# A long-convolution and MLP kernel: second transform stages in 64-row tiles, in-place products, 32x32 turns on VectorE, a 128-row last stage and a token-major gate

## The chip, the cores and the metric

The kernel runs on one core of a Trainium2 chip. The metric is device microseconds of one execution; of several executions the median is given. The engines are named as the profile names them: PE (TensorE matmul) with PEld (its weight loads), DVE (VectorE), ACT (ScalarE), POOL (GpSimd) and SP (SyncE, which issues DMAs).

## The reference

All tensors are bf16, S = 2048 tokens, D = 512 channels, a hidden width of 1376. Cut to what matters:

```
h  = x + LN(x) * y            # x = A_q, LN without scale and shift
kv = shift_conv(k, 4 taps) * v
y  = causal_conv(kv, ssm_k) + kv * ssm_D     # per channel, length 2048, by FFT in fp32
h2 = h + relu(LN(h) @ w1) @ w2
```

The reference pads the convolution to 4096 points, takes real FFTs of kv and ssm_k along the tokens, multiplies them and transforms back; the first 2048 results are y.

## The kernel before

Everything is on chip; the work is a chain of stages, and the program order of each engine is written out by hand (`manual_schedule`), so an instruction waits for everything in front of it on its own engine. PSUM and SBUF tiles come from pools with a fixed number of buffers; a tile's next use waits for the last reader of the old one.

The transform of a channel's 2048 tokens, t = 64 a + b, is done in two matmul stages at odd frequencies. `to_rows` (L220) turns the channel-major input so that the 32 values of a lie on partitions: 64 transposes of 128x128 on PE, evacuated by DVE and ACT in turns. `stage1` (L226) contracts over a in four 32-row tiles that run side by side (tile_position 32 rg), with a bf16 high and a bf16 low part of the sine table, and writes 64 columns: 32 frequencies k1, real and imaginary. For x (not for k) it streams 128 columns, of which the upper 64 are zeros (`wide`). Its results go to `a1k` and `a1x`, with partitions (d, b): d is a half of a 128-channel group. Between the stage-1 groups of k, `taps` (L272) makes the four-tap shift convolution as matmuls with diagonal matrices `wdiag` and DVE multiplies with v.

`stage2` (L243) contracts over b with 128x128 tables `cc`, `cs`, `cn` (cosine, sine, minus sine) that are block diagonal in d: half of each table is zeros. For k it gives the real part and the imaginary part separately into `kf`; the real part gets ssm_D added (L306). For x the `product` (L328) multiplies both parts with both parts of kf, split 176 to 80 channels between DVE (from PSUM) and POOL (from a copy that ACT makes), and `finish` (L346), two steps behind, sums the four products on PE with plus and minus identity matrices into `psy`, which ACT copies back into kf. A step handles two k1; there are 16.

`inv1` (L474) contracts over the second frequency with `dre` and `dim`, 16 blocks of eight N=256 matmuls, evacuated by ACT and DVE into `ax`. Beside it lie the tables of the last stage (`ec_turns`, `ec_wrap`, `ec_sins`), the first LayerNorm (`ln1_stats`, `ln1_norm`), DMA transposes of x and of LN(x) into channel-major `xT` and `qT` (`lift`, `rows_T`), and the subtraction of the mean over D from w1 (`column_means`, `center`), which stands in for the mean of the second LayerNorm. `inv2` (L531) is the last stage: 512-column groups of channel-major results from 32-row tiles, four side by side, 128 matmuls for each quarter q. `gate` (L522) multiplies with qT and adds xT, all channel-major, so `mlp1` takes its result straight from SBUF; a DMA transpose brings the sum back to token-major `xh` for the residual. `mlp1` and `mlp2` follow for each quarter, with inv2 of a later quarter between them.

Of the kernel before, what the change touches and what calls it, by code (L numbers as in the profile page):

```python
# [20 lines left out]
class _Pools:  # L21
# [13 lines left out]
    def pop(self, name):  # L35
        self.open.pop(name).__exit__(None, None, None)
# [5 lines left out]
def _turns(nc, out, r, col, M, quarter):  # L42

    nc.vector.tensor_scalar(out=out, in0=r, scalar1=col, scalar2=float(M // 2 + (M // 4 if quarter else 0)),
                            op0=ALU.mult, op1=ALU.add)
    nc.vector.tensor_single_scalar(out=out, in_=out, scalar=M - 1, op=ALU.bitwise_and)


def _tokens(src2d, t0, nt):

    D = src2d.shape[1]
    return [bass.AP(tensor=src2d.tensor, offset=src2d.offset + (16 * a + t0) * D, ap=[[64 * D, 32], [1, nt * D]])
            for a in range(4)]
# [3 lines left out]
def kernel(  # L57
# [22 lines left out]
    lo, hi = slice(0, 64), slice(64, 128)  # L80
    halves = (lo, hi)
# [4 lines left out]
    slotA = pl.push("slotA")  # L86
    vp = pl.push("vp")
    early = pl.push("early")
    wp = pl.push("wp", side="right")
    kvp = pl.push("kvp", side="right")  # L90
# [3 lines left out]
    sk = early.tile([P, DC, S], BF16, name="sk")  # L94
# [3 lines left out]
    dtab = consts.tile([P, 64, DC], BF16, name="dtab")  # L98
    draw = consts.tile([P, DC, 64], BF16, name="draw")
    for dp in range(2):  # L100
        src = bass.AP(tensor=A_ssm_D.tensor, offset=A_ssm_D.offset + 64 * dp, ap=[[0, 64], [P, DC], [1, 64]])
        nc.scalar.dma_start(out=draw[64 * dp:64 * dp + 64, :, :], in_=src)
    vT = vp.tile([P, DC, S], BF16, name="vT")
    CH = 512
    kT = [(kvp if c < 2 else early).tile([P, DC, CH + 16], BF16, name=f"kT{c}") for c in range(4)]
    wdiag = kvp.tile([P, DC, KS, P], BF16, name="wdiag")

# [10 lines left out]
    nbias = consts.tile([P, 1], F32, name="nbias")  # L118
    pbias = consts.tile([P, 1], F32, name="pbias")
    nc.vector.memset(nbias[:], -0.5 * TURN)  # L120
    nc.vector.memset(pbias[:], 0.5 * TURN)
    eps_t = consts.tile([P, 1], F32, name="eps_t")
    nc.vector.memset(eps_t[:], EPS)

    hsc = consts.tile([P, 2], F32, name="hsc")
    hbi = consts.tile([P, 2], F32, name="hbi")
    for t_, v_ in ((hsc, TURN / 8192), (hbi, -0.5 * TURN)):
        nc.vector.memset(t_[:], 0.0)
        for dp in range(2):
            nc.vector.memset(t_[halves[dp], dp:dp + 1], v_)  # L130
# [6 lines left out]
    n1i = early.tile([P, 1], I32, name="n1i")  # L137
    for s in range(0, P, 32):
        nc.gpsimd.iota(n1i[s:s + 32, :], pattern=[[0, 1]], base=0, channel_multiplier=1)
    r1 = early.tile([P, 32], I32, name="f1_r")  # L140
# [4 lines left out]
    r2 = early.tile([P, 32, 64], I32, name="w_r")  # L145
    nc.gpsimd.iota(r2[:], pattern=[[2, 32], [128, 64]], base=1, channel_multiplier=0)
    r3 = early.tile([P, 64], I32, name="dm_r")
    nc.gpsimd.iota(r3[:], pattern=[[1, 64]], base=0, channel_multiplier=0)
# [5 lines left out]
    n1c = early.tile([P, 1], F32, name="n1c")  # L154
    n2c = early.tile([P, 1], F32, name="n2c")
    nc.vector.tensor_copy(out=n1c[:], in_=n1i[:])
    nc.vector.tensor_copy(out=n2c[:], in_=n2i[:])

    t1 = early.tile([P, 64], I32, name="f1_t")
    _turns(nc, t1[:, 0:32], r1[:], n1c[:], 128, True)  # L160
    _turns(nc, t1[:, 32:64], r1[:], n1c[:], 128, False)
    f1f = early.tile([P, 64], F32, name="f1_f")
    _sin(f1f[:, 0:32], t1[:, 0:32], 128)
    _sin(f1f[:, 32:64], t1[:, 32:64], 128, neg=True)


    def pieces(name, *sizes):
        got, at = [], 0
        for i, n in enumerate(sizes):
            got.append((at, wp.tile([P, n, P], F32R, tag=f"{name}{i}", name=f"{name}{i}")))  # L170
            at += n
        return got

    cc, cs, cn = pieces("c2c", 16, 16), pieces("c2s", 22, 10), pieces("c2n", 8, 8, 8, 8)

    def at_k1(tab, k1):
        a, t = [p for p in tab if p[0] <= k1][-1]
        return t[:, k1 - a, :]

    tsn = early.tile([P, 32, 64], I32, name="w_ts")  # L180
    _turns(nc, tsn[:], r2[:], n2c[:], 8192, False)

    def table(dst, turns):
        for a, t in dst:
            for dp in range(2):
                nc.scalar.activation(out=t[:, :, 64 * dp:64 * dp + 64], in_=turns[:, a:a + t.shape[1], :], func=ACT.Sin,  # L186
                                     scale=hsc[:, dp:dp + 1], bias=hbi[:, dp:dp + 1])

    table(cs, tsn)
    f1hi = consts.tile([P, P], BF16, name="f1_hi")  # L190
    f1lo = consts.tile([P, P], BF16, name="f1_lo")
    for f in (f1hi, f1lo):
        nc.gpsimd.memset(f[:, 64:128], 0.0)
    nc.vector.tensor_copy(out=f1hi[:, 0:64], in_=f1f[:])
    f1d = early.tile([P, 64], F32, name="f1_d")
    nc.vector.tensor_tensor(out=f1d[:], in0=f1f[:], in1=f1hi[:, 0:64], op=ALU.subtract)
    nc.vector.tensor_copy(out=f1lo[:, 0:64], in_=f1d[:])
    _turns(nc, r2[:], r2[:], n2c[:], 8192, True)
# [3 lines left out]
    for a, b in ((0, 8), (8, 16), (16, 22), (22, 24), (24, 32)):  # L202
        (ao, to), (ai, ti) = [[p for p in tab if p[0] <= a][-1] for tab in (cn, cs)]
        nc.gpsimd.tensor_single_scalar(out=to[:, a - ao:b - ao, :], in_=ti[:, a - ai:b - ai, :].bitcast(F32), scalar=-1.0,  # L204
                                       op=ALU.mult)


    nc.gpsimd.tensor_copy(out=dtab[:], in_=draw[:].rearrange("p r g -> p g r"))

# [16 lines left out]
    def stage1(fl, a_out, gb, engs, wide=False):  # L226

        pss = [bank2("ps1") for _ in range(2)]
        outs = [pss[rg // 2][:, rg % 2, :] for rg in range(4)]
        for gi in range(8):  # L230
            for f, first in ((f1hi, True), (f1lo, False)):
                for rg in range(4):
                    rows = slice(32 * rg, 32 * rg + 32)
                    w = 128 if wide and gi < 7 else 64
                    nc.tensor.matmul(out=outs[rg][:, 64 * gi:64 * gi + w],  # L235
                                     lhsT=fl[rows, 8 * gb + gi, :, :].rearrange("p d n -> p (d n)"),
                                     rhs=f[rows, 0:w], start=first, stop=not first,
                                     tile_position=(32 * rg, 0), skip_group_check=True)
        for h in range(2):
            copy(engs[h], a_out[:, :, 32 * gb:32 * gb + 32].rearrange("p c (g r) -> p c g r", r=DC)[:, :, :, 2 * h:2 * h + 2],  # L240
                 pss[h][:].rearrange("p r (g c) -> p c g r", c=64))

    def stage2(ps, a_in, kp, s):  # L243

        for kk in range(2):
            k1 = 2 * kp + kk
            w_re, w_im = ((cc, cs), (cn, cc))[s]
            nc.tensor.matmul(out=ps[:, kk, :], lhsT=at_k1(w_re, k1), rhs=a_in[:, k1, :], start=True, stop=False,  # L248
                             skip_group_check=True)
            nc.tensor.matmul(out=ps[:, kk, :], lhsT=at_k1(w_im, k1), rhs=a_in[:, 32 + k1, :], start=False, stop=True,  # L250
                             skip_group_check=True)


    kfl = early.tile([P, 64, 2, 64], BF16, name="kfl")
    skv = sk[:].rearrange("p c (a b) -> p c a b", b=64)
    for q in range(8):
        to_rows(skv, q, kfl, "DADADADA"[q])
    table(cc, r2)

    t3 = early.tile([P, 2, 64], I32, name="dm_t")  # L260
    _turns(nc, t3[:, 0, :], r3[:], n2c[:], 64, True)
    _turns(nc, t3[:, 1, :], r3[:], n2c[:], 64, False)
    dsc = early.tile([P, 2, 64], F32, name="dm_f")
    _sin(dsc[:], t3[:], 64)
    dre = consts.tile([P, 2, 2, 64], F32R, name="dre")
    dim = consts.tile([P, 2, 2, 64], F32R, name="dim")
    nc.gpsimd.memset(dre[:].bitcast(F32), 0.0)
    nc.gpsimd.memset(dim[:].bitcast(F32), 0.0)
    a1k = slotA.tile([P, 64, 256], F32R, tag="A", name="a1k")

# [9 lines left out]

    for gb in range(8):
# [82 lines left out]
    for kp in range(16):  # L364
        product(kp)
        if kp >= LAG:
            finish(kp)
# [277 lines left out]
```

## Time and profile before

| what | value |
|---|---|
| median of 3 runs | 232.25 us (232.03 to 232.39) |
| span of the profiled execution | 230.8 us; the median of the runs lies 1.45 us above it |
| mean granted TensorE clock | 0.974 of full speed |
| busy: PE, PEld, DVE, ACT, POOL | 201.4, 142.4, 142.9, 118.1, 78.3 us |
| matmuls | 2544, each with a weight load |
| DMA | 20.10 MB, 49194 packets |

The span runs from the first to the last instruction of one execution. Busy time is the time in which an engine has at least one instruction under way; matmuls are pipelined, so their mean duration (N=512: 0.38 us) is longer than the distance from one to the next (0.23 us). A line of the groups gives line number, engine, operation, out<-in, shapes, count, then busy us and mean ns of one, then the idle time of the engine just before them with what ended most of it.

### The profile page before, as it was taken

How to read it: one execution, taken by the hardware profiler on the slowest of the kernel's cores; microseconds unless marked ns; L12 is line 12 of the kernel's file. 1: busy time of each engine (PE TensorE's matmuls, PEld its weight loads, DVE VectorE, ACT ScalarE, POOL GpSimd, SP SyncE). 2: the span in 40 equal slices, each digit the busy share in tenths (PEclk: the TensorE clock that was granted, in tenths of full speed). 3: DMA queues.
4: the chain of work that ended last, by engine and by line, in shares of the span. 5: the costliest groups of instructions: out<-in, count | busy, mean ns of one | idle time of the engine just before them, and what ended most of it. 6: DMA issues, size and time to landing. Idle time of an engine off the chain costs nothing.

```text
span 230.8 us, 5978 instructions
## 1 busy us (share of the span) xinstructions
PE 201.4 (87%) x2544; PEld 142.4 (62%) x2544; DVE 142.9 (62%) x214; ACT 118.1 (51%) x177; POOL 78.3 (34%) x108
## 2 busy tenths in 40 slices
PE   0485999899966699999898889999999999999991
PEld 0473454899955699998787775444744474444440
DVE  7974667676664589998685869583971346134031
ACT  3789766555585478888486501750162026206400
POOL 6399910000000599998860770400220002002000
PEclk9999999999999589999999997999999999999998
DMA  6999920000000000772962168977244214021011
GB/s 197 306 230 161 169 60 3 0 4 0 0 7 6 3 1 0 182 244 77 211 119 53 33 214 127 213 140 114 54 91 96 55 37 91 6 59 27 3 46 46
DMA packets 49194, 20.10 MB, mean 87 GB/s; under 512 B 44208, under 2 KB 47632, under 8 KB 49168
## 3 DMA queue, kind: packets, MB, share of 16 engines
q1 hardware_dynamic: 46688, 18.24, 37.7%
q10 hardware_dynamic: 2480, 1.48, 2.4%
q8 instruction: 20, 0.33, 0.6%
q14 instruction: 6, 0.05, 0.1%
HBM read 7.08 MB, written 2.10 MB: 40 GB/s over the span
## 4 chain that ended last, share of the span: by engine, by line
PE 78%; ACT 8%; DMA 4%; DVE 4%; POOL 3%; issue 2%; POOLq 0%
PE ps1m L552 17%; PE ps2m L565 16%; PE pz L540 7%; PE psy L351 6%; PE pst L223 5%; PE pkv L276 5%; PE u L248 4%; PE u L250 4%; DMA sk<-in_A_ssm_k_dram 4%; PE ps2k L248 3%; PE ps2k L250 3%; PE ps L235 3%; ACT a1x L213 3%; PE psi L479 2%; ACT c2c L186 2%
## 5 line engine op out<-in xcount | busy, mean ns | idle before, releaser
L554 ACT ACTIVATE h1T<-ps1m 128x512 bf16<-128x512 f32 (+1 forms) x44 | 26.0, 596 | 57.6 <-PE ps1m L552 57.6
L552 PE MATMUL ps1m<-xT,w 128*128 128x512 bf16 (+1 forms) x176 | 40.3, 390 | 0.0
L565 PE MATMUL ps2m<-w,h1T 128*128 128x512 bf16 (+1 forms) x176 | 38.7, 379 | 0.0
L568 DVE SCALAR_TENSOR_TENSOR o<-ps2m,rstd,xh 128x512 bf16<-128x512 f32 x16 | 12.0, 750 | 38.8 <-PE ps2m L565 38.7
L552 PEld LDWEIGHTS <-w 128*128 128x128 bf16 (+1 forms) x176 | 17.8, 102 | 21.1 <-issue 2.2
L341 DVE TENSOR_TENSOR t<-u,kf 128x704 fp32r<-128x704 f32 x32 | 27.1, 888 | 5.3 <-ACT usb L337 5.3
L341 POOL TENSOR_TENSOR t<-usb,kf 128x320 fp32r<-128x320 f32 x32 | 28.6, 923 | 4.2 <-ACT usb L337 3.2
L565 PEld LDWEIGHTS <-h1T 128*128 128x128 bf16 (+1 forms) x176 | 17.2, 98 | 20.7
L429 POOL TENSOR_SCALAR rstd<-mv 128x4 f32<-128x4 f32 x8 | 1.9, 241 | 66.4 <-DVE mv L427 66.3
L425 DVE BATCH_NORM_STATS2 st<-xh 128x6 f32<-128x512 bf16 x32 | 19.7, 676 | 0.0
L213 ACT CAST kf<-psy 128x512 fp32r<-128x512 f32 x30 | 17.5, 643 | 1.8 <-PE psy L351 0.2
L540 PE MATMUL pz<-ecore,ax 32*128 32x256 f32 (+7 forms) x512 | 15.7, 274 | 2.1 <-ACT ax L213 1.1
L540 PEld LDWEIGHTS pz<-ecore,ax 32*128 32x128 f32 x512 | 15.2, 185 | 3.4 <-issue 2.1
L276 PE MATMUL pkv<-kT,wdiag 128*128 128x512 bf16 x64 | 15.2, 380 | 1.6 <-POOL c2n L204 1.2
L479 PE MATMUL psi<-dre,kf 128*128 128x256 f32 x64 | 16.0, 290 | 0.4 <-ACT ax L213 0.4
L351 PE MATMUL psy<-t,ipos 128*128 128x512 f32 x48 | 15.8, 390 | 0.0
L321 POOL CAST ipos<-ident 128x128 fp32r<-128x128 bf16 x1 | 0.3, 289 | 45.5 <-ACT a1x L213 45.5
L213 ACT CAST a1k<-ps 128x1024 fp32r<-128x1024 f32 x13 | 13.0, 1068 | 5.4 <-PE ps L235 5.4
L279 DVE TENSOR_TENSOR vT<-pkv,vT 128x1024 bf16<-128x1024 f32 x8 | 9.8, 1225 | 9.4 <-PE pkv L276 9.2
L479 PE MATMUL psi<-dim,kf 128*128 128x256 f32 x64 | 15.5, 283 | 0.0
L213 ACT CAST ax<-psi 128x1024 fp32r<-128x1024 f32 x12 | 11.7, 1012 | 7.3 <-PE psi L479 4.3
L223 PE MATMUL pst<-ident,sk 128*128 128x128 bf16 x64 | 6.7, 293 | 9.2 <-DMA sk<-in_A_ssm_k_dram 9.2
(110 smaller groups left out, 410.9 us busy)
## 6 DMA issues: line engine op xcount, KB each, us to landing
sk<-in_A_ssm_k_dram SPq DMA_DIRECT2D x1, 2048.0 KB, 8.5
xh<-in_A_q_dram SPq DMA_DIRECT2D x16, 128.0 KB, 3.2
out_dram<-o SPq DMA_DIRECT2D x64, 32.0 KB, 1.6
w<-in_B_w_dram SPq DMA_DIRECT2D x1, 1376.0 KB, 6.0
w<-in_B_w_dram ACTq DMA_DIRECT2D x1, 1280.0 KB, 6.5
w<-in_B_w_dram ACTq DMA_DIRECT2D x1, 96.0 KB, 6.3
draw<-in_A_ssm_D_dram ACTq DMA_DIRECT2D x2, 32.0 KB, 8.4
kT<-in_A_k_dram SPq DMA_TRANSPOSE x4, 6.8
```

Of the source, the lines that this page charges most:

```text
L213: nc.scalar.copy(out=o, in_=i)
L223: nc.tensor.transpose(out=pst[:, 0, i, :], in_=src[:, :, :, 8 * q + i], identity=ident[:])
L248: nc.tensor.matmul(out=ps[:, kk, :], lhsT=at_k1(w_re, k1), rhs=a_in[:, k1, :], start=True, stop=False, skip_group_check=True)
L276: nc.tensor.matmul(out=ps[:, i, :], lhsT=wdiag[:, 2 * h + i, j, :], rhs=kT[c][:, 2 * h + i, 16 - j:CH + 16 - j], start=(j == 0), stop=(j = ...
L341: eng.tensor_tensor(out=t[:, :, j, :], in0=in0.unsqueeze(1).to_broadcast([P, 2, n, 2]), in1=kfr[:, :, j, ks], op=ALU.mult)
L351: nc.tensor.matmul(out=psy[:], lhsT=m_[:], rhs=t_.rearrange("p j k -> p (j k)"), start=first, stop=not first)
L425: nc.vector.bn_stats(out=st[:, i, :], in_=src[:, i, :])
L479: nc.tensor.matmul(out=ps[:, i // 2, i % 2, :], lhsT=kf[:, c, 4 * m:4 * m + 4, :].rearrange("p r k -> p (r k)"), rhs=d[:].rearrange("p d a ...
L540: nc.tensor.matmul(out=pz[:, rg, j:j + w, :].rearrange("p a b -> p (a b)"), lhsT=ax[rows, 64 * rho + n2, :, :].rearrange("p d g -> p (d g) ...
L552: nc.tensor.matmul(out=ps1[:fsz, :].rearrange("p (i t) -> p i t", i=4), lhsT=w1[:, c, fc * P:fc * P + fsz], rhs=hT[sc][:, :, c, :], start= ...
L554: nc.scalar.activation(out=h1T[:fsz, fc, :], in_=ps1[:fsz, :], func=ACT.Relu)
L565: nc.tensor.matmul(out=ps2[:], lhsT=h1T[:ksz, fc, i * P:(i + 1) * P], rhs=w2[:ksz, fc, :], start=(fc == 0), stop=(fc == NFC - 1))
```

## The change

Every stage from the tables to the gate is rewritten; `taps`, `to_rows`, `mlp1` and `mlp2` keep their matmuls.

- **Tables.** One table `tab` holds, for each k1, four blocks of 64 columns (two sines, and their negatives by POOL) on 64 rows for each d. The phases are made in four pieces through one buffer `ta`. wdiag is made on POOL after the negatives; before, it was made ahead of them.
- **ssm_D** enters as a spike at token 0 of the kernel: four more 32-row matmuls for each stage-1 group of k (`spike`), instead of the add at L306.
- **Stage 1 of x** streams 64 columns, and follows the transposes of v directly; the second stage of k moves behind it, into the product loop, two steps ahead.
- **Second stages.** 64-row tiles, one for each d; an output has real and imaginary part on its 128 partitions, so the zeros are gone. `order` swaps the two parts for the second product.
- **Products.** One 128x1024 multiply of each output with k's, written over a1x and a1k. DVE makes the first; the second is POOL's (from ACT's copy) in even steps and DVE's in odd ones. `finish` is gone.
- **Inverse stage.** It contracts over (part, frequency) and sums the two sources in PSUM, 16 blocks of four N=512 matmuls; DVE turns each block in 32x32 squares and ACT copies it into a1x. The tables of this stage (`wd`) and of the last one (`tf`) are made ahead of its first block.
- **Last stage.** 128-row matmuls, 16 of N=256 for each quarter, with tokens on partitions. The gate works token-major; a DMA transpose then makes `hT` for mlp1. The DMA transposes of x and LN(x) are gone.
- **Loads.** x (four DMAs) and w1 are issued by SP ahead of the product. The centering of w1 goes to POOL wholly, from copies by ACT.

The core of the diff, new lines (`...` stands for what is left out):

```
for i in range(2):
    if i:
        nc.gpsimd.iota(r2[:], pattern=[[2, 16], [128, 64]], base=33, channel_multiplier=0)
    for b, o in enumerate((4096.0, 6144.0)):
        ta = early.tile([P, 16, 64], I32, tag="ta", name="ta", bufs=1)
        _turns(ta[:], r2[:], n2c[:], 8192, o)
        _sin(tab[:, 16 * i:16 * i + 16, b, :], ta[:], 8192)
for i in range(4):
    nc.gpsimd.tensor_single_scalar(out=tab[:, 8*i:8*i+8, 2:4, :], in_=tab[:, 8*i:8*i+8, 0:2, :].bitcast(F32), scalar=-1.0, op=ALU.mult)
wdiag = rows.tile([P, DC, KS, P], BF16, name="wdiag")
...
def second(ps, a_in, kp, order):
    for i in range(2):
        k1 = 2 * kp + i
        for c in range(2):
            for d in range(2):
                rw = slice(64 * d, 64 * d + 64)
                b = 1 - c + order
                nc.tensor.matmul(out=ps[:, d, 256 * i:256 * i + 256],
                                 lhsT=tab[rw, k1, b:b + 2, :].rearrange("p b k -> p (b k)"), rhs=a_in[rw, c, k1, :],
                                 start=(i == 0 and c == 0), stop=(c == 1), tile_position=(64 * d, 0), ...)
def second_k(kp):
    ps = bank2("ps2k")
    second(ps, a1k, kp, 0)
    nc.scalar.copy(out=spot(a1k, kp), in_=ps[:])
def product(kp, pool):
    u2 = bank2("u")
    second(u2, a1x, kp, 1)
    u1 = bank2("u")
    second(u1, a1x, kp, 0)
    kk = spot(a1k, kp)
    if pool:
        usb = prod.tile([P, 2, 512], F32, tag="usb", name="usb", bufs=2)
        nc.scalar.copy(out=usb[:], in_=u1[:])
    nc.vector.tensor_tensor(out=spot(a1x, kp), in0=u2[:], in1=kk.bitcast(F32), op=ALU.mult)
    (nc.gpsimd if pool else nc.vector).tensor_tensor(out=kk, in0=(usb if pool else u1)[:], in1=kk.bitcast(F32), op=ALU.mult)
second_k(0)
second_k(1)
for kp in range(16):
    if kp < 14:
        second_k(kp + 2)
    product(kp, kp % 2 == 0)
...
for i in range(3):
    _turns(t3[:], r3[:], n2c[:], 64, ow[i][:])
    _sin(w3[:, i, :], t3[:], 64)
nc.vector.tensor_single_scalar(out=wd[:], in_=w3[:], scalar=1.0 / 2048, op=ALU.mult)
def inv_block(d, c0):
    ps = bank2("pz")
    for b in range(2):
        for m, src in ((1, a1k), (0, a1x)):
            nc.tensor.matmul(out=ps[:, b, :], lhsT=wd[:, m:m + 2, :].rearrange("p b k -> p (b k)"),
                             rhs=src[:, d, 16 * b:16 * b + 16, c0:c0 + 32], start=(m == 1), stop=(m == 0))
    zs = mid.tile([P, 32, 32], F32, tag="zs", name="zs", bufs=3)
    nc.vector.transpose(out=zs[:], in_=ps[:].rearrange("p b (k c) -> p c (b k)", c=32))
    nc.scalar.copy(out=a1x[:, d, :, c0:c0 + 32], in_=zs[:].rearrange("p c n -> p n c"))
...
nc.gpsimd.memset(tf[:, :, 1].bitcast(F32), 0.0)
rf = mid.tile([P, 4, 2, 32], I32, name="rf")
for j in range(0, NT, 4):
    nc.gpsimd.iota(rf[:], pattern=[[1, 4], [16, 2], [64, 32]], base=j, channel_multiplier=0)
    nc.gpsimd.tensor_scalar(out=rf[:], in0=rf[:], scalar1=k1o[:], scalar2=ofc[:], op0=ALU.mult, op1=ALU.add)
    nc.vector.tensor_single_scalar(out=rf[:], in_=rf[:], scalar=8191, op=ALU.bitwise_and)
    for a in range(2):
        nc.scalar.activation(out=tf[:, j:j + 4, 0:3:2, a, :], in_=rf[:], func=ACT.Sin, ...)
...
for i in range(16):
    inv_block(i // 8, 32 * (i % 8))
    if i in (1, 3, 5, 7):
        column_mean(i // 2)          # 4 matmuls, ACT copy, POOL subtract
    if i == 9:
        stats(xh[0], mv1, rstd1, 0)
...
def last(q):
    pz = psz.tile([P, 4, D], F32, tag="pz", name="pz")
    for i in range(4):
        j = 4 * q + i
        for d in range(2):
            for t in range(2):
                nc.tensor.matmul(out=pz[:, i, :].rearrange("p (r d g) -> p d r g", r=DC, d=2)[:, d],
                                 lhsT=tf[:, j, t:t + 2].rearrange("p t a n -> p (t a n)"),
                                 rhs=a1x[:, d, 16 * t + j, :].rearrange("p (r g) -> p r g", r=DC), ...)
def gate(q):
    nc.vector.tensor_tensor(out=qn[q][:], in0=pzs[q][:], in1=qn[q][:], op=ALU.mult)
    nc.vector.tensor_tensor(out=xh[q], in0=qn[q][:], in1=xh[q], op=ALU.add)
    nc.sync.dma_start_transpose(out=hT[q][:].rearrange("p i r t -> p (i r) t"), in_=xh[q].rearrange("p i d -> p (i d)"))
...
ln1_norm(0); last(0); gate(0); stats(xh[1], mv1, rstd1, 1); ln1_norm(1); last(1); gate(1)
stats(xh[0], mv2, rstd2, 0); mlp1(0); stats(xh[2], mv1, rstd1, 2); ln1_norm(2); last(2); mlp2(0); gate(2); ...
```

The memsets of small constant columns (`ow`, `k1o`, `of`, `hsc`, `hbi`) and `ofc` stand between `wd` and the loop over j. `iota` and the `tensor_scalar` on POOL are those of the snippet; `ones` is set on POOL behind that loop.

More of the change, by code (lines that the diff above doesn't have):

```diff
@@ L163 @@
+    _turns(t1[:, 32:64], r1[:], k1c[:], 128, 64.0)
+    f1f = early.tile([P, 64], F32, name="f1f")
     _sin(f1f[:, 0:32], t1[:, 0:32], 128)
     _sin(f1f[:, 32:64], t1[:, 32:64], 128, neg=True)
[L167 to L198, printed above, removed]
+    f1hi = consts.tile([P, 64], BF16, name="f1hi")
@@ L201 @@
                                 in1=wsh[:, rg, :].unsqueeze(2).to_broadcast([P, KS, P]), op=ALU.mult)
[L202 to L208, printed above, removed]
+    xfl = rows.tile([P, 64, 2, 64], BF16, name="xfl")
+    pl.pop("early")
     def copy(eng, o, i):
@@ L232, in stage1 @@
                 for rg in range(4):
[L233 to L237, printed above, removed]
+                    rw = slice(32 * rg, 32 * rg + 32)
+                    nc.tensor.matmul(out=outs[rg][:, gi, :],
+                                     lhsT=fl[rw, 8 * gb + gi, :, :].rearrange("p d n -> p (d n)"),
+                                     rhs=f[rw, :], start=first and not spike, stop=not first,
                                      tile_position=(32 * rg, 0), skip_group_check=True)
+        oc = a_out[:].rearrange("p c k (r g) -> p (c k) g r", r=DC)
         for h in range(2):
-            copy(engs[h], a_out[:, :, 32 * gb:32 * gb + 32].rearrange("p c (g r) -> p c g r", r=DC)[:, :, :, 2 * h:2 * h + 2],
+            copy(engs[h], oc[:, :, 8 * gb:8 * gb + 8, 2 * h:2 * h + 2],
                  pss[h][:].rearrange("p r (g c) -> p c g r", c=64))
[L243 to L269, printed above, removed]
     def taps(c, h):
@@ L513 @@
+    pl.pop("mid")
+    pl.pop("psF")
+    pl.pop("a1kp")
+    mp = pl.push("mp", side="right")
+    psz = pl.push("psZ", space=PSUM)
+    psm = pl.push("psM", bufs=4, space=PSUM)
     w2 = mp.tile([P, NFC, D], BF16, name="w2")
```

425 lines of the change are left out of this document (145 added, 280 removed).

## The prediction

> **What bounds the kernel now.** I read the page's parts 1 and 4 first.
>
> ```profile
> PE 201.4 (87%) x2544; PEld 142.4 (62%) x2544; DVE 142.9 (62%) x214; ACT 118.1 (51%) x177; POOL 78.3 (34%) x108
> ...
> PE 78%; ACT 8%; DMA 4%; DVE 4%; POOL 3%; issue 2%; POOLq 0%
> ```
>
> TensorE is busy 87% of the span and is 78% of the chain that ended last, so a cut in its work counts only where it is the last to finish. I therefore cut the span where the chain changes its line, and asked for the busy time of each stretch (columns: PE, PEld, DVE, ACT, POOL; then the granted clock).
>
> ```profile
> 17.00:41.20 24.20, 20.13 (x577) 10.54 (x578) 14.61 (x15) 17.62 (x18) 12.28 (x16) 1.00 0.62 97
> 41.20:47.10 5.90, 5.90 (x65) 5.90 (x66) 3.67 (x3) 3.74 (x4) 0.00 (x0) 1.00 0.00 0
> 47.10:62.50 15.40, 15.40 (x134) 15.27 (x136) 10.65 (x9) 7.43 (x8) 0.00 (x0) 1.00 0.01 2
> 62.50:77.00 14.50, 8.68 (x513) 7.32 (x513) 7.47 (x7) 11.08 (x11) 0.79 (x2) 0.95 0.02 5
> 77.00:82.40 5.40, 5.40 (x25) 5.40 (x26) 3.80 (x5) 1.46 (x5) 3.77 (x5) 0.51 0.02 3
> 82.40:109.80 27.40, 27.32 (x169) 24.14 (x167) 24.01 (x29) 23.81 (x57) 24.88 (x28) 1.00 0.37 108
> 109.80:131.40 21.60, 18.29 (x148) 17.12 (x148) 15.65 (x27) 14.18 (x17) 12.14 (x20) 1.00 0.51 100
> 131.40:140.40 9.00, 7.98 (x257) 7.74 (x258) 6.82 (x14) 0.00 (x0) 5.72 (x6) 0.99 0.57 166
> 140.40:226.00 85.60, 85.60 (x608) 42.42 (x608) 41.33 (x81) 28.24 (x48) 7.63 (x12) 0.98 0.40 78
> ```
>
> In order these are taps with stage 1 of k, transposes of v, second stage of k, stage 1 of x, product (two rows: its first 5.4 us at clock 0.51), inverse stage, two last stages, then MLP with the other two, PE-bound to the end. PE fills its row except in stage 1 of x (8.68 of 14.50) and the inverse (18.29 of 21.60). The prices come from the groups by form (mean ns is the last figure before the second bar):
>
> ```profile
> L213 ACT CAST a1x<-ps 128x1024 fp32r<-128x1024 f32 x10 | 10.1, 1074 | 3.3 <-PE ps L235 3.3
> ...
> L306 DVE TENSOR_TENSOR kf<-ps2k,dtab 128x1024 fp32r<-128x1024 f32 x8 | 9.8, 1225 | 4.7 <-PE ps2k L250 4.7
> ...
> L308 ACT CAST kf<-ps2k 128x1024 fp32r<-128x1024 f32 x8 | 8.1, 1014 | 8.0 <-PE ps2k L250 8.0
> ...
> L540 PE MATMUL pz<-ecore,ax 32*128 32x256 f32 x288 | 10.0, 283 | 2.1 <-ACT ax L213 1.1 <-issue 1.0
> ...
> L204 POOL TENSOR_SCALAR c2n<-c2s 128x1024 fp32r<-128x1024 f32 x3 | 8.3, 2792 | 0.1
> ...
> L200 POOL TENSOR_TENSOR wdiag<-ident,wsh 128x512 bf16<-128x512 bf16 x4 | 4.5, 1152 | 4.8 <-DMA wsh<-in_A_shift_k_dram 4.8
> ```
>
> A mean is an upper price. In the timeline a row of back-to-back ones has a shorter pitch: three ACT a1x take 2.89 us (0.92 each after the first), two DVE a1x 2.36 (1.14).
>
> **The change, in order of time.** Marks are us from the span's start. The profiled span is 230.8; the median is 232.25, so 1.45 lie around it and I add them at the end. A measurement can tell about 0.2% (0.46 us) from no change.
>
> *Front (before: v transposes start at 41.16).* The tables halve in size (4096 sines a partition, not 8192), and the 4.53 us of c2c sines that the chain holds at 16.9 go. But one buffer `ta` now makes DVE and ACT take turns: a turn is 1.3 (half of the 128x2048 pair, 1.28 + 1.23), a sine 1.23 (128x1024 row), four rounds 10.1, from 5.8 (the f1 sines and their three DVE operations now go ahead) to 16. DVE beside the POOL negations costs more: dm_t took 0.75 and 0.97 there against 0.24 and 0.20 later, so +1.3; the last sine ends at 17.5. Two of the four POOL negations (2.79 each) wait for it, and wdiag is queued behind them: 17.6 + 5.6 + 1.15 = 24.4 for the first taps. The rounds are PE's: 8 x 1.84 taps, 7 x 0.61 stage 1, 7 x 0.12 for the four spike matmuls (a set of four 32-row matmuls of up to 256 columns takes 0.12 at pz: 3.81 us for 32 sets) = 19.8. PE has stood idle before, so some at half clock: 0 to 1.9, I take 1.0. With the last vT (1.24) the transposes start at 46.6: **+5.4**.
>
> *v and stage 1 of x.* The transposes stay 5.94, to 52.5. The last xfl copy (1.3) was hidden by the second stage of k, which no longer follows; its cover is gone: 53.9. Stage 1 narrows to 64 columns (0.61 us a group, the kfl row), so its 16 evacuations bound it: walking the four two-bank buffers with 0.92 and 1.14 gives 10.2 to the last copy and 11.3 to the first u2. PE works half the time there; for a clock drop I add 1.2. First product operation at 66.4.
>
> *Second stages and product (before: 15.4 of ps2k and 32.8 of product).* A step of two k1 now has 24 matmuls of 64 rows and 256 columns. No row shows 64-row tiles; the bounds are 0.12 a pair if two run side by side as four 32-row ones do (pz), and 0.24 if not (ps2k: 0.12 each). I take 0.12, the row with the same mechanism: 1.44 a step. Per two steps ACT has three 128x1024 copies (3 x 0.92 = 2.8), POOL one multiply (0.92 us for 320 elements at L341, so 2.9), DVE three 128x1024 multiplies with a PSUM operand (L306's form, pitch 1.15 = 3.45). DVE is last. With four buffers the next u2 waits for the last multiply plus two tiles (0.16): 3.6 for two steps, 28.8 in all. Filling adds 1.2, the last steps without second_k give 0.3 back, half clock costs 0.5: **product ends at 96.6**, against 109.8. The four psy matmuls of a step (0.92) and their ACT copies are gone into the inverse stage, which sums both sources in PSUM.
>
> *Head of the inverse stage (before: 1.8 us).* The table work stands in program order ahead of the first turn. On DVE: r3 from POOL (1.2, behind its last multiply), three rounds of turns (0.48) and sine (0.35) on one t3 (2.65), wd (0.2); then 14 memsets and ofc (1.3); then four `and` that each wait for POOL (iota 0.35, multiply 0.37) and, by one buffer rf, for two sines (0.95): rounds of 2.07. tf's memset on POOL (about 1.1, four times dre's 0.30) lies ahead of the first. Sum 13: behind the fourth `and` sit all 16 turns, behind the eighth sine all ACT copies. PE fills four buffers and stops. First turn at 109.6.
>
> *Inverse loop.* PE needs 4 x 0.23 (N=512, psy) = 0.92 a block, ACT about 0.95. The 32x32 turn is in no row. Bounds: 0.63 (half the 2048-element integer row, SBUF only; then ACT's 0.95 binds, -4) and 2.29 (L523, as if two passes; +17). I take 1.22, the 128x1024 PSUM-to-SBUF copy of the same engine: 19.5. Statistics on DVE add 2.8, the last copy 1.1. The first column mean stops PE until POOL reaches `ones`, and blocks 2 and 3 then come at half clock: 1.8. Sum 25.2, to **134.8** (before: 131.4). [...]
>
> *Last stage, gate, MLP.* last(0) is 16 x 0.12 = 1.9 (before 3.8 for 32 sets of four). The gate is 2.29 + 1.23. New on the path is the transpose of its result: mlp1(0) took xT from SBUF at once, now hT comes by DMA. The same form ran at L528:
>
> ```profile
> DMA to landing us min/median/max: 4.3/4.6/5.0
> ```
>
> So 134.8 + 1.9 + 3.5 + 4.6 = 144.8 for mlp1(0), against 140.4. The MLP has the same matmuls: 11.25 (its first, cold then too) + 3 x 9.57 + 4 x 9.51 + 2 x 1.92 = 81.9 against 85.6, and the tail 4.76. Later hT transposes have a whole mlp stage before their use.
>
> *Costed at nothing.* x and w1 loads now issue before the product, some 40 us early (3.2 and 6.0 to land). Eight transposes leave SP's queue, none is put ahead of hT. Four tiny drow loads replace two on ACT ahead of the sine table (1.88 for the two). All four w1 centerings go to POOL (2.83 each), done by the 13th block; uncovered, they would hold mlp1(0). Four wm copies on ACT (0.4) fit in its slack.
>
> Sum: 144.8 + 81.9 + 4.8 = 231.5, + 1.45 = **233.0 us**. Front +5.4, xfl +1.3, stage 1, second stages and product -19.9, head and loop +16.6, last and gate +1.0, MLP -3.7: the gain of the product is spent in the two table chains.
>
> **Rivals.**
> - *Clock stays up (faster).* Place: every gap that I priced. It decides at what idle time the clock falls. For it: gaps of 1.3 us at 19.6 and 21.4 left it at 1.00, and 9.2 us with nothing at the start too. Against: after 2.3 idle us at 74.7 it was 0.51 until 82.4, and after one gap of 1.0 at 137.4 0.50. Price: 1.0 + 1.2 + 0.5 + 1.8 = 4.5, and 1.65 of the cold mlp1(0): 226.9 to 228.5. [...]
> - *Turns take two passes*: 2.29 each, +17: 250. Nothing in the profile excludes it.
> - *64-row tiles run one by one*: PE 2.88 a step, 46 instead of 28.8: 250. Against it stand pz and the L235 rows, four abreast.
> - *Half clock through the product*, because PE pauses in every step: 24 x 0.21/2 = 2.5 a step, +11: 244. Against it: stage 1 of x, 60% busy, kept 0.95.
> - *The step list is right but hand-offs that I put at nothing add up*: 236 to 242.
>
> **Chances.** Forecast case 231 to 236: 0.42. Clock stays up, 226.5 to 231: 0.29. Two passes 0.05, one by one 0.04, half clock 0.04, hand-offs 0.12, and 0.04 for a shorter turn (229). Below 231.8 lie 0.29 + 0.04 and 0.05 of the forecast case: faster 0.38. Within 231.8 to 232.7: 0.10. Slower 0.52. The range 227.5 to 242 leaves out 0.05 below and the 0.13 of the three large cases.
>
> **What would show it.** Right: first taps near 24 behind POOL's negations, v transposes near 46.6, DVE the fullest engine of the product at 3.6 us per two steps, 12 to 14 us between the last multiply and the first turn with PE mostly idle, a DMA wait ahead of mlp1(0). Wrong: taps before 21, PE as the product's bound, a turn far from 1.2 us, or turns that start before tf is done.

## The result, and the profile after

The changed kernel takes 262.32 us (median of 4 runs, 262.01 to 262.67) against 232.3 us for the kernel before in the same job: 1.133 times as long, 95% interval 1.127 to 1.140. Forecast were 233.0 us, 227.5 to 242: the time lies far outside. The profiled execution spans 260.6 us at a mean granted clock of 0.869 (before: 230.8 and 0.974). Medians in us, here and below, are of all executions of a kernel; ratios to the kernel before leave out executions in a slower state that some of them show, and since the experiments ran in several jobs, the ratio is what compares across them.

Parts 1 and 4 of the page of the changed kernel:

```profile
PE 188.8 (72%) x2116; PEld 119.8 (46%) x2128; DVE 153.0 (59%) x226; ACT 143.8 (55%) x137; POOL 67.3 (26%) x70
...
PE 46%; ACT 27%; DVE 14%; POOL 5%; issue 4%; DMA 2%; ACTq 1%; DVEq 0%; POOLq 0%; SPq 0%
```

TensorE has 12.6 us less to do than before, and its share of the chain has gone from 78% to 46%. ACT went from 8% to 27%: the chain now runs through its copies. Cut by stage (PE, PEld, DVE, ACT, POOL, then granted clock):

```profile
24.70:51.40 26.70, 22.03 (x532) 11.46 (x540) 15.71 (x11) 22.24 (x13) 2.95 (x3) 0.94 0.21 36
...
58.70:82.30 23.60, 13.66 (x556) 11.81 (x558) 12.42 (x6) 21.28 (x13) 0.00 (x0) 0.51 0.29 64
82.30:114.80 32.50, 25.79 (x344) 21.91 (x342) 28.74 (x26) 20.63 (x21) 19.05 (x8) 0.97 0.23 66
114.80:129.50 14.70, 3.93 (x9) 2.62 (x10) 4.86 (x35) 4.34 (x9) 5.12 (x14) 0.50 0.01 2
129.50:162.50 33.00, 20.45 (x74) 12.89 (x72) 23.29 (x28) 32.89 (x22) 12.68 (x6) 0.81 0.08 27
162.50:174.20 11.70, 7.14 (x30) 6.70 (x31) 6.76 (x12) 0.00 (x0) 1.28 (x2) 0.59 0.38 90
174.20:260.60 86.40, 81.52 (x380) 39.10 (x383) 41.84 (x81) 26.30 (x44) 7.60 (x12) 0.98 0.21 43
```

These are taps with stage 1 of k, stage 1 of x, product, head, inverse loop, last stage with gate and hT, and MLP. The head is the time between the last multiply of the product and the first turn, a turn is one of the 32x32 transposes of the inverse loop, and kfl and xfl are what `to_rows` makes for k and for x. ACT fills its row in stage 1 of x (21.28 of 23.60) and wholly in the loop (32.89 of 33.00), with 13 and 22 instructions. The groups by form tell how long one takes (mean ns ahead of the second bar):

```profile
L333 ACT CAST a1x<-zs 128x1024 fp32r<-128x1024 f32 x16 | 30.9, 2002 | 0.1
L194 ACT CAST a1k<-ps 128x1024 fp32r<-128x1024 f32 x13 | 23.9, 1967 | 5.3 <-PE ps L225 5.3
...
L332 DVE STREAM_TRANSPOSE zs<-pz 128x1024 f32<-128x1024 f32 x16 | 19.6, 1239 | 6.7 <-ACT a1x L333 4.4 <-PE pz L329 2.3
...
L194 ACT CAST a1x<-ps 128x1024 fp32r<-128x1024 f32 x10 | 18.6, 2210 | 2.9 <-PE ps L225 2.9
...
L288 ACT CAST a1k<-ps2k 128x1024 fp32r<-128x1024 f32 x16 | 16.5, 1084 | 2.6 <-PE ps2k L277 2.6
...
L196 DVE CAST a1x<-ps 128x1024 fp32r<-128x1024 f32 x6 | 12.4, 2109 | 6.1 <-PE ps L225 6.1
```

One engine and one form, 128x1024 with 1024 elements a partition, at two prices: 1.08 us at L288, 2.0 to 2.2 us at L333 and L194; DVE shows 2.11 where the kernel before had 1.22:

```profile
L215 DVE CAST a1x<-ps 128x1024 fp32r<-128x1024 f32 x6 | 7.2, 1222 | 6.2 <-PE ps L235 5.4 <-ACT kf L308 0.8
```

The tile's shape and the type are the same, and L194 and L288 both read PSUM (L333 reads SBUF); what differs is the order in which the elements lie in SBUF. At L194 the copy walks over the channel block r innermost, and in the new layout of a1k and a1x two neighbours in r lie 256 bytes apart, so that every 4-byte element is written alone; at L333 zs is read in steps of 128 bytes. In the kernel before every such SBUF run held at least two neighbours.

### The profile page after: what moved, and what is told of

The parts are those of the page before. It is cut to its first block, busy times and chain, and to the rows that moved or that the text cites. A ratio compares the mean times of both kernels' runs of the same rounds, so it can differ in the third digit from the quotient of the medians.

```text
span 260.6 us, 4958 instructions
## 1 busy us (share of the span) xinstructions
PE 188.8 (72%) x2116; PEld 119.8 (46%) x2128; DVE 153.0 (59%) x226; ACT 143.8 (55%) x137; POOL 67.3 (26%) x70
## 3 DMA queue, kind: packets, MB, share of 16 engines
q1 hardware_dynamic: 29472, 14.05, 24.4%
## 4 chain that ended last, share of the span: by engine, by line
PE 46%; ACT 27%; DVE 14%; POOL 5%; issue 4%; DMA 2%; ACTq 1%; DVEq 0%; POOLq 0%; SPq 0%
PE ps1m L447 15%; PE ps2m L458 15%; ACT a1x L333 11%; ACT a1x L194 6%; ACT a1k L194 4%; DVE a1x L299 4%; PE pkv L238 4%; PE u L277 4%; PE pz L429 3%; PE pst L205 2%; POOL tab L182 2%; DVE a1k L300 2%; ACT tab L125 2%; DMA hT<-xall 2%; PE ps L225 2%
## 5 line engine op out<-in xcount | busy, mean ns | idle before, releaser
L447 PE MATMUL ps1m<-hT,w 128*128 128x512 bf16 (+1 forms) x176 | 40.3, 390 | 2.2 <-DMA hT<-xall 2.2
L300 POOL TENSOR_TENSOR a1k<-usb,a1k 128x1024 fp32r<-128x1024 f32 x8 | 19.1, 2388 | 68.1 <-DVE a1x L299 68.1
L333 ACT CAST a1x<-zs 128x1024 fp32r<-128x1024 f32 x16 | 30.9, 2002 | 0.1
L194 ACT CAST a1k<-ps 128x1024 fp32r<-128x1024 f32 x13 | 23.9, 1967 | 5.3 <-PE ps L225 5.3
L277 PE MATMUL u<-a1x,tab 64*128 64x256 f32 x256 | 22.2, 304 | 4.0 <-DVE a1x L299 2.9
L299 DVE TENSOR_TENSOR a1x<-u,a1k 128x1024 fp32r<-128x1024 f32 x16 | 19.4, 1220 | 8.6 <-PE u L277 7.8
L332 DVE STREAM_TRANSPOSE zs<-pz 128x1024 f32<-128x1024 f32 x16 | 19.6, 1239 | 6.7 <-ACT a1x L333 4.4
L329 PE MATMUL pz<-a1k,wd 128*128 128x512 f32 x32 | 15.9, 496 | 10.0 <-DVE wd L323 6.4
L277 PEld LDWEIGHTS u<-a1x,tab 64*128 64x128 f32 x256 | 18.1, 197 | 7.5 <-DVE a1x L299 4.3
L429 PE MATMUL pz<-a1x,tf 128*128 128x256 f32 x64 | 12.4, 362 | 11.4 <-DVE zs L332 5.6
L194 ACT CAST a1x<-ps 128x1024 fp32r<-128x1024 f32 x10 | 18.6, 2210 | 2.9 <-PE ps L225 2.9
L372 DVE BATCH_NORM_STATS2 st<-xall 128x6 f32<-128x512 bf16 x32 | 19.6, 676 | 0.0
L288 ACT CAST a1k<-ps2k 128x1024 fp32r<-128x1024 f32 x16 | 16.5, 1084 | 2.6 <-PE ps2k L277 2.6
```

The source lines that it names most:

```text
L194: nc.scalar.copy(out=o, in_=i)
L277: nc.tensor.matmul(out=ps[:, d, 256 * i:256 * i + 256], lhsT=tab[rw, k1, b:b + 2, :].rearrange("p b k -> p (b k)"), rhs=a_in[rw, c, k1, :] ...
L299: nc.vector.tensor_tensor(out=spot(a1x, kp), in0=u2[:], in1=kk.bitcast(F32), op=ALU.mult)
L300: (nc.gpsimd if pool else nc.vector).tensor_tensor(out=kk, in0=(usb if pool else u1)[:], in1=kk.bitcast(F32), op=ALU.mult)
L332: nc.vector.transpose(out=zs[:], in_=ps[:].rearrange("p b (k c) -> p c (b k)", c=32))
L333: nc.scalar.copy(out=a1x[:, d, :, c0:c0 + 32], in_=zs[:].rearrange("p c n -> p n c"))
```

## Experiments

Theory: the copies lose their speed where the elements that they touch in SBUF one after the other are single (not in runs of two or more), and that is most of the 29 us. Rivals: the head and the other table chains; the half clock (0.51 in stage 1 of x); contention.

### The copies, one at a time

**e1_g_inner.** The copies of stage 1 walk r outside and g inside: eight neighbours in SBUF, with strided reads of PSUM.

```
-oc = a_out[:].rearrange("p c k (r g) -> p (c k) g r", r=DC)
-copy(engs[h], oc[:, :, 8*gb:8*gb+8, 2*h:2*h+2], pss[h][:].rearrange("p r (g c) -> p c g r", c=64))
+oc = a_out[:].rearrange("p c k (r g) -> p (c k) r g", r=DC)
+copy(engs[h], oc[:, :, 2*h:2*h+2, 8*gb:8*gb+8], pss[h][:].rearrange("p r (g c) -> p c r g", c=64))
```

> Edit: the stage-1 copies of the changed kernel go over the channels g innermost instead of the pair r, so each SBUF write is a run of 8 neighbouring 4-byte elements instead of single ones 256 bytes apart; layout and result stay. Lone-element theory (ACT and DVE take two element times for an SBUF access whose consecutive 4-byte elements stand alone): the copies fall from 1.97 to 2.2 us to the 1.07 (ACT) and 1.22 (DVE) of before; taps become PE-bound again (v transposes at 46.5 to 48 instead of 51.4), stage 1 of x to the first u2 takes 12 to 14 us instead of 23.6; total 246 to 250. Rival (the copies are slow for the number of loop levels or for the read of PSUM across banks): a change of the read order could help too, so this run alone does not exclude it; if neither holds, 262.

**e2_pair_layout.** The layout becomes (g r), written in pairs as in the kernel before, with PSUM read in the changed kernel's order; the last stage then reads a1x with a step of 16 bytes.

```
-rearrange("p c k (r g) -> p (c k) g r")   +rearrange("p c k (g r) -> p (c k) g r")     # stage1
-rhs=a1x[...].rearrange("p (r g) -> p r g")  +rhs=a1x[...].rearrange("p (g r) -> p r g")  # last
```

> Edit: a1k and a1x keep channel order (g r) as in the kernel before, so the copies write pairs of neighbouring elements; the order in which PSUM is read is that of the changed kernel. The last stage then reads its moving operand with a step of 4 elements. Lone-element theory: a pair is enough, 1.07 and 1.22 us as before; 246 to 251. PSUM-read rival: the read is unchanged, so 1.97 to 2.2 us and 262. If TensorE pays for the step of 16 bytes too, the last stage's matmuls show it: 0.24 us from one to the next instead of 0.12.

**e3_read_whole.** In the inverse loop ACT reads zs from front to back and writes the single elements, in place of the reverse: `copy(out=a1x[:, d, :, c0:c0+32].rearrange("p n c -> p c n"), in_=zs[:])`.

> Edit: ACT's copy behind the 32x32 turn reads the turned block in its own order (contiguous) and writes single elements 1 KB apart, instead of reading single elements 128 bytes apart and writing runs of 32. Lone-element theory: either side pays, 2.0 us a copy, loop 33 us, 262. Rival (only the read side pays): 1.0 us a copy, DVE sets the loop with 1.24 a block, about 25 us; 254.

**e4_pair_turn.** DVE writes its turned block as pairs, ACT reads with a step of 8 bytes and writes runs of 32.

```
+zs = mid.tile([P, 16, 32, 2], ...)
+nc.vector.transpose(out=zs[:].rearrange("p m c t -> p c m t"), in_=...)
+nc.scalar.copy(out=a1x[:, d, :, c0:c0+32].rearrange("p (m t) c -> p m t c", t=2), in_=zs[:].rearrange("p m c t -> p m t c"))
```

> Edit: DVE writes the turned block with pairs of neighbouring elements (tile 16 x 32 x 2), and ACT's copy reads it with a step of 8 bytes, so that two consecutive reads fall within 16 bytes; it writes runs of 32 as before. Lone-element theory: ACT 1.0 us, DVE 1.24; the loop of 33 us falls to 25 to 26 (DVE-bound, as the prediction had it), total 254 to 255.5. Rivals: the turn itself pays for writing pairs (2.2 us a block, loop 36, 265); or a step of 8 bytes is as bad as one of 128 (ACT 2.0, 262). [...]

Measured: 253.14 (ratio to the kernel before 1.094, 1.087 to 1.101), 257.85 (1.115, 1.106 to 1.123), 261.73 (1.130, 1.123 to 1.137) and 252.91 us (1.092, 1.086 to 1.099). The groups by form of the four, in this order:

```profile
L194 ACT CAST a1x<-ps 128x1024 fp32r<-128x1024 f32 x10 | 9.6, 1018 | 4.8 <-PE ps L225 4.7
L196 DVE CAST a1x<-ps 128x1024 fp32r<-128x1024 f32 x6 | 7.3, 1222 | 6.5 <-PE ps L225 6.4
```
```profile
L429 PE MATMUL pz<-a1x,tf 128*128 128x256 f32 x64 | 16.6, 436 | 11.4 <-DVE zs L332 5.6 <-ACT a1x L333 3.4 <-DVE qln L436 2.4
...
L194 ACT CAST a1x<-ps 128x1024 fp32r<-128x1024 f32 x10 | 10.2, 1097 | 3.8 <-PE ps L225 3.7
```
```profile
L333 ACT CAST a1x<-zs 128x1024 fp32r<-128x1024 f32 x16 | 29.7, 1989 | 0.1
```
```profile
L332 DVE STREAM_TRANSPOSE zs<-pz 128x1024 f32<-128x1024 f32 x16 | 18.9, 1224 | 2.4 <-PE pz L329 2.4
...
L333 ACT CAST a1x<-zs 128x1024 fp32r<-128x1024 f32 x16 | 18.1, 1136 | 4.4 <-DVE zs L332 4.3
```

e1 saves 9.2 us, not the 12 to 16 that the theory gave it: its copies are as short as expected, but stage 1 of x still takes 17.0 us where 12 to 14 were expected, for a reason found below. Runs of two are enough (e2: 2.21 to 1.10 us with the PSUM side untouched), a single element costs the same whether it is read or written (2.00 us read in the changed kernel, 1.99 written in e3), and pairs cost the turn on DVE nothing (1.224 us, 1.239 in the changed kernel). e2 also shows that TensorE pays for a step of 16 bytes in what it streams: its four last stages keep TensorE busy for 16.6 us in place of the changed kernel's 12.4 (436 and 362 ns in the mean), and on the chain 16 of its matmuls take 3.73 us, not 1.91. That is why e2 missed its 246 to 251, though its first multiply comes 2.1 us earlier than e1's. A step of 8 bytes is nearly free in ACT's copy behind the turn (1.14 us in e4, against 2.00 with the step of 128 bytes); the price of single elements is here a factor of 1.7 to 2.2.

**e5_both_copies.** e1 and e4 together.

> Both layouts of e1_g_inner and e4_pair_turn together, nothing else changed. Theory (the copies with single 4-byte elements cost 9.2 us in the stages ahead of the product and 9.4 us in the inverse loop, two stretches that do not touch): the savings add, 262.3 - 9.2 - 9.4 = 243.7, range 242.5 to 245.5. Rival (part of the saving of the one is the wait of the other, for example because an earlier product lets the head start colder): less than 15 us, over 247.

244.78 us (1.058, 1.052 to 1.063), within the expected range. In ratios e1 saves 0.039 and e4 0.041, and both together 0.076, so within the intervals they add. So 17.5 of the 30 us are the copies.

**e8_before_single.** The cause put into the kernel before, alone, in its 16 copies of stage 1 of x:

```
+oc = a_out[:].rearrange("p c (r g) -> p c g r", r=DC)      # shortened; was "p c (g r) -> p c g r"
```

> The kernel before, with one part of the change alone: the 16 copies of stage 1 of x write a1x with the channel index turned, so that neighbours in PSUM land 256 bytes apart in SBUF, single 4-byte elements where there were pairs (the channels come out in another order; nothing else is changed). Theory (price is on the side of SBUF, whatever the kernel): ACT a1x 1.07 to about 2.0 to 2.2 us, DVE a1x 1.15 to about 2.1, stage 1 of x 12.5 to 21 us or more, total 8 to 13 us longer: 240 to 245. Rival (the long copies of the changed kernel come from PE or POOL working beside them, or from the half clock): the copies stay within 1.1 and 1.3 us, total within 1 us of the kernel before.

```profile
L213 ACT CAST a1x<-ps 128x1024 fp32r<-128x1024 f32 x10 | 18.8, 2133 | 0.1
...
L215 DVE CAST a1x<-ps 128x1024 fp32r<-128x1024 f32 x6 | 12.1, 2078 | 6.1 <-PE ps L235 5.3 <-ACT kf L310 0.8
```

The price moves with the order, in a kernel that has nothing else of the change, so the order as the cause of the long copies is shown. The time, 237.29 us (1.028, 1.023 to 1.033), is 6.4 more than the kernel before, less than the 8 to 13 expected: from the first matmul of the stage to the first multiply it went from 16.2 to 21.7 us, and the 2.1 us in which TensorE had waited there for nothing that the profile shows are gone under the longer copies: its row has none, but 4.7 us of waits for ACT's copies. What those waits go with, e9 and e11 tell.

### Program order

**e6_front.** e5 with wdiag ahead of the negations on POOL and `ta` with two buffers. **e7_tables_early.** e6 with wd and tf taken out of the head: constants behind the taps, then in the product loop, behind `product(kp)` of kp = 1, 3, 5, 7 and 9, one `and` on DVE and the two sines on ACT that wait for it.

> e5_both_copies with the diagonal weights made on POOL ahead of the table negatives, and two buffers ta. Theory (the front of 24.7 us is the chain of table rounds and then POOL's queue): the four wdiag instructions end near 15, the copies of kfl near 18, first taps at 19 to 21 against 24.7, and 3.5 to 5.5 us less than e5_both_copies: 238 to 240. [...]

> e6_front with the tables of the inverse and the last stage (wd, tf) made in pieces behind the taps and in the product loop, one buffer usb for lack of room. Theory (the head of 14.7 us is this table work in program order): first turn 1.5 to 3.5 us after the last multiply of the product; the product grows by 1 to 3 us since DVE is its fullest engine; the clock is near 1 in the loop; 9 to 13 us less than e6_front: 226 to 231. Rival (the head is there because POOL's last multiply and the first four blocks of PE are late, not for the tables): 5 us or more stay, gain under 8 us.

e6: 242.51 us (1.050, 1.043 to 1.057), 2.3 less where 3.5 to 5.5 were expected: first taps at 22.6 and not at 19 to 21, since the copies of kfl queue behind the tables on DVE and ACT (TensorE waited 4.2 us for one on DVE). e7: 238.69 us (1.036, 1.027 to 1.046), 3.8 less where 9 to 13 were expected. The head does vanish (last multiply to first turn 14.7 us in e6, 1.0 in e7), so it was table work; but the product grew from 32.4 to 42.3 us. ACT in the timeline of e7 (start, length, in brackets the idle time before):

```profile
78.97 1.02 ACT L308 CAST a1k<-ps2k 128x1024 fp32r<-128x1024 f32 x1
83.06 1.09 ACT L341 ACTIVATE tf<-rf,hbi,hsc 128x256 fp32r<-128x256 int32 x2 [3.07 <-DVE rf L339]
84.06 0.99 ACT L308 CAST a1k<-ps2k 128x1024 fp32r<-128x1024 f32 x1
```

The sines are 1.1 us of work, but ACT waited 3.1 us for the `and` (1.8 the later times), which stands behind DVE's multiplies; the copy that the next step needs stood behind the sines. The wait was moved, not taken away. The edit also leaves only one buffer `usb`, for lack of room: two steps with sines take 5.6 us, the next two without them 4.4 against 4.03 in the changed kernel, with ACT waiting 0.7 us for POOL to free that buffer. So a small part of the 9.9 us is the buffer's.

### Half clock, or TensorE standing still

In e5 stage 1 of x still took 19.5 us to the first multiply (in a profiled execution 2.3 us above its median), where the prediction's walk has 12.5.

**e9_wide.** e5 with `rhs=f[rw, 0:128]` in stage 1 of x (upper half zeros), so that TensorE is busier. **e11_half_stream.** e5 with stage 1 of x leaving out the f1lo matmuls: its values lose the low part of the sine table.

> e5_both_copies with stage 1 of x streaming 128 columns, the upper 64 of them zeros, as the kernel before did: more work for TensorE, the same results. Theory (the clock falls in this stage because TensorE is idle half of the time, and the fall costs more than the copies: 19.5 us from 55.7 to the first multiply of the product where 16 copies alone need 10 to 12): the clock stays at 0.95 or more as in the kernel before, the stage takes 12 to 14 us, total 5 to 7 us less: 238 to 240. Rival (the stage is bound by its copies and the hand-off of the four PSUM buffers, at any clock): within 1.5 us of e5_both_copies, or longer.

> e5_both_copies with stage 1 of x leaving out the matmuls of the low part of the sine table (256 instead of 512 matmuls and as many weight loads fewer; the values lose precision, all else is the same). e9_wide left 18.0 us from the first matmul of this stage to the first product at a high clock, and TensorE stood still there three or four times for 0.9 to 1.5 us, once after every 128 matmuls with their weight loads, with no releaser. Theory (TensorE's own instruction stream cannot be delivered at the rate of these short matmuls): with half the instructions half of the stops go, and the work between them too; the stage falls from 19.5 to 13 to 15 us, total 4 to 6.5 us less than e5_both_copies: 238.5 to 241. Rival (the stage waits for the hand-off between the 16 copies and the four PSUM buffers, and the stops lie in the shade of these waits): within 2 us of e5_both_copies.

e9: 244.91 us (1.051, 1.044 to 1.058), no change clear of noise. The clock over most of the stage rose from 5 to 6 tenths in e5 (the slices of its page from 55 to 74 us) to 0.89, and it still took 18.0 us; the 5 to 7 us that the theory gave to the half clock aren't there, and it fell. e11: 238.69 us (1.038, 1.031 to 1.044), by its ratio 4.6 us less than e5, as expected, and 13.1 us for the stage, although the clock was 0.5 in it (the slices of its page from 53 to 65 us). PE in the timeline of e9, its waits without a releaser (`<-issue`):

```profile
61.88 0.21 PE L228 MATMUL ps<-f1lo,xfl 32*128 32x64 bf16 x4 [1.15 <-issue]
...
65.61 0.21 PE L228 MATMUL ps<-f1lo,xfl 32*128 32x64 bf16 x4 [1.18 <-issue]
...
69.61 0.21 PE L228 MATMUL ps<-f1lo,xfl 32*128 32x64 bf16 x4 [1.45 <-issue]
```

They come 3.7 to 4 us apart, after every 128 matmuls with their 128 weight loads, and with a first one of 0.3 they sum to 4.1 us; in e5 to 6.1, in the changed kernel to 2.2 (it is slower there anyway), in e11 to none. The rows of e5 and e11:

```profile
L225 PE MATMUL ps<-f1lo,xfl 32*128 32x64 bf16 x256 | 7.4, 225 | 6.1 <-issue 6.1
```
```profile
L225 PE MATMUL ps<-f1hi,xfl 32*128 32x64 bf16 x256 | 5.8, 234 | 3.9 <-ACT a1x L194 2.1 <-DVE xfl L196 1.4 <-DVE a1x L196 0.2
```

The kernel before has them too, and its row showed it:

```profile
L235 PE MATMUL ps<-f_lo,xfl 32*128 32x128 bf16 x224 | 7.6, 215 | 2.1 <-issue 2.1
```

That they are gone when half of these matmuls and weight loads are left out is shown. By the count alone one or two would have stayed, so they seem to belong to short matmuls at full pace: stage 1 of k in e5, with as many matmuls but the taps between them, has none (e10 has one of 0.9 us there). That it is the delivery of TensorE's instructions is argued, not shown: the page lists a DMA queue of kind instruction with 16 packets and 0.26 MB, 16 KB each, and from kernel to kernel the packets follow the instructions (5978 and 20 in the kernel before, 4958 and 16 in the changed one, 4446 and 14 in e11, so 255 and 256 instructions for each packet more), and 128 matmuls with their 128 weight loads are 256 instructions too. No view ties a stop to a packet.

### A version that beats both

**e10_reordered.** Both layouts of e5, 128 columns in stage 1 of x, and the table work put where its engine waits anyway and its inputs are ready: wdiag first on POOL; tab half ahead of the transposes of k, half between the taps; all phases of tf at once, its sines behind the later taps and, with no wait, in the product; x loaded behind the product; the last even step on DVE. **e12_trimmed.** e10 with the constant columns at the very front, wd in stage 1 of x, and the first gate with its transpose in two halves.

> Both copies of e5_both_copies, 128 columns in stage 1 of x, and the table work spread anew: on POOL wdiag first; half of tab ahead of the transposes of k and half between the taps; phases of tf in one piece on POOL and DVE at the front, its sines two by two on ACT behind the later taps and, with nothing to wait for, in the product; wd between the taps; x loaded behind the product (to make room); the last even product step wholly on DVE. Theory (what the changed kernel lost is the copies, program order and the half clock that follows from them, and its stages as such are shorter than those of the kernel before): first taps at 16 to 19, transposes of v at 37 to 41, 12 to 14 us for stage 1 of x, 30 to 32 for the product, 1.5 to 3 for the head, 24 to 25.5 for the loop, mlp1 at 130 to 138, total 217 to 226, below the 230.9 of the kernel before. Rival (as in e7_tables_early, each piece of table work that is put beside other work holds up a queue there by as much as it saved): 232 or more.

> e10_reordered with three hold-ups moved: the small constant columns are set on DVE at the very front and no longer between the copies of kfl (2.6 us there); the six small phase operations of wd and its sine go from the taps into stage 1 of x (TensorE waited 1.4 us behind them); the first gate and its DMA transpose are made in two halves of two tiles. Theory (each of these sits ahead of a copy or transfer that TensorE waits for): first taps 1 to 2 us earlier, transposes of v 2.5 to 4 us earlier, mlp1 after the last copy of the loop in 9 to 10 us instead of 12.2; 4 to 7 us less than e10_reordered's profiled run of 225.9, 219 to 222. Rival (the transfer takes its 4 to 5 us whatever its size, and TensorE catches up on what was late): within 2 us of e10_reordered, 224 to 228.

e10: 228.43 us (0.978, 0.972 to 0.985); e12: 225.38 us (0.980, 0.975 to 0.984, from six runs). Both beat the kernel before, by some 2%. Both missed their own forecasts (217 to 226 and 219 to 222): in e10 the head (1.5 us) and the loop (25.0) came as expected, but the front, stage 1 of x (15.9) and the product (34.1) took longer. e12 is no faster than e10 in its ratio, so its rival held. The windows of e12 from the first taps on (taps, v, stage 1 of x, product, head, loop, last stage, MLP):

```profile
20.80:44.00 23.20, 20.77 (x536) 10.72 (x540) 16.36 (x16) 16.69 (x19) 9.23 (x4) 1.00 0.47 70
44.00:51.40 7.40, 5.96 (x65) 5.85 (x67) 4.90 (x4) 4.05 (x4) 0.00 (x0) 1.00 0.00 0
51.40:69.10 17.70, 11.60 (x552) 9.88 (x552) 8.54 (x13) 11.85 (x14) 0.69 (x1) 1.00 0.10 25
69.10:103.20 34.10, 26.77 (x346) 22.30 (x346) 29.82 (x25) 22.23 (x25) 16.97 (x9) 0.99 0.21 61
103.20:104.60 1.40, 1.26 (x3) 1.11 (x4) 0.00 (x0) 0.00 (x0) 0.00 (x0) 0.50 0.95 222
104.60:130.00 25.40, 19.93 (x78) 13.39 (x77) 22.59 (x28) 19.39 (x20) 12.59 (x6) 0.90 0.16 32
130.00:140.40 10.40, 6.87 (x31) 6.53 (x32) 6.53 (x13) 0.02 (x1) 0.39 (x2) 0.69 0.71 186
```

The head is 1.4 us and the product kept its pace of 4.03 us for two steps (34.1 with the step that went to DVE). Stage 1 of x is still 17.7 us at full clock, with 5.1 us of waits without a releaser. The front missed what was expected: first taps come at 20.8, 1.6 us later than in e10 and not 1 to 2 earlier, and TensorE waited 2.3 us for a copy of kfl on DVE.

## Why the prediction was wrong

By its steps, predicted and then measured in us:

| step | predicted | measured |
|---|---|---|
| first taps, behind POOL's negations | 24.4 | 24.7 |
| taps and stage 1 of k | 22.2 | 26.7 |
| transposes of v, last xfl copy | 7.3 | 7.3 |
| stage 1 of x to the first multiply | 12.5 | 23.6 |
| product | 30.2 | 32.4 |
| head of the inverse stage | 13.0 | 14.7 |
| inverse loop | 25.2 | 33.0 |
| last stage, gate, hT | 10.0 | 11.7 |
| MLP and tail | 86.7 | 86.4 |

The step that failed is a price: "walking the four two-bank buffers with 0.92 and 1.14" and, in the loop, "ACT about 0.95". Both were read from rows of the same shape, and here not the shape but the order of the elements in SBUF set the price of a copy. They measured 2.0 to 2.2 us on ACT and 2.1 on DVE. The same price stands unsaid behind "The rounds are PE's", which holds only while the copies of a1k are short. Most of three rows of the table rests on it: with short copies 3.0 to 3.2 of the 4.5 us in the taps were gone (e5, e1) and 6.6 of the 11.1 in stage 1 of x (e1), and the loop took 24.0 to 25.0 us (e5, e4) against the 25.2 predicted. e5 took these copies back and saved 17.5 us; e8 made them in the other kernel.

The second part is smaller and was in the views: the walk of stage 1 left out the waits without a releaser, 2.1 us in the row of the kernel before. Without them, and with half of the matmuls, the walk came out: in e11 the stage took 13.1 against 12.5. For the clock I had put 1.2 us there, and no run measures that term alone: e9 raises the clock and the work together, and its stage differs from e5's by 1.5 us and its stops by 2.0. That the clock's fall to 0.51 isn't what made the stage long is shown by e11, 13.1 us at 0.5, beside e12, 17.7 at 1.00. What e5 still lies above the forecast, 12 us, is spread over stage 1 of x, the taps, the product, the head and the last stage.

The rest held: first taps behind POOL's negations, the head as table work in program order (its `and` come every 2.56 us and not 2.07, which is most of the 1.7 us in that row), the turn at 1.24 us (1.22 taken), 64-row tiles two abreast (in the timeline of the changed kernel eight of them end 0.74 us after the first one's start, and one alone takes 0.28), the transfer ahead of mlp1, the MLP. In the product DVE is the fullest engine as predicted, but two steps take 4.03 and not 3.6 us: three multiplies fill 3.6, and DVE then waits 0.4 for TensorE where 0.16 in all was taken. Of the rivals none was this case: I had none in which a copy grows dearer.

What stays open: what the stops are and why they differ so much between kernels (0.3 to 2.6 us each), and how much the clock takes in head and last stage, where it was never raised alone (the first last stage took 3.4 us, where 1.9 was taken and the window shows a clock of 0.59).

## What to carry over

Take the price of a copy only from a row with the same element order on its SBUF side: single 4-byte elements cost 1.7 to 2.2 times as much here, in reading (2.00 us) as in writing (1.99), and pairs in writing next to nothing (1.10 us on ACT in e2, 1.02 in runs of eight in e1), while the order in which PSUM was read moved it by less than 0.1 us (the same two rows). When work is moved between others' steps, ask what stands behind it in its own queue and whether its input is ready there. Where hundreds of short matmuls follow each other, count the waits without a releaser of the nearest such row.

## What the runs showed of the hardware that I had not expected

- A copy of 128x1024 in fp32 takes 1.97 to 2.2 us on ACT and 2.1 on DVE with single elements on the SBUF side, against 1.02 to 1.10 and 1.22 with pairs or longer runs (1.14 on ACT with a step of 8 bytes).
- TensorE pays too for a step of 16 bytes in its streamed operand: 436 ns in place of 362 for N=256 in the mean, and 3.73 us in place of 1.91 for 16 of them on the chain.
- A turn in 32x32 squares takes 1.22 to 1.24 us, what a plain copy of that size from PSUM takes on DVE (1.22), with pairs as output too (1.22).
- In stage 1 of x TensorE stopped for 0.3 to 2.6 us at a time, 128 matmuls and 128 weight loads apart or a multiple of that, in all kernels here but e8 and e11 (one stop of 2.2 us in the changed kernel, 6.1 us in all in e5). It did not where half of them are left out (e11), nor in e8, where it waited 4.7 us for longer copies.
